# An attention kernel planned step by step: new load order for the first batch, a new rule for the weights' copies, the last pair of heads in two parts

## The chip, the cores and the metric

The kernel runs on one core of one Trainium2 chip. The metric is the device time of one execution in microseconds; the median over runs is compared. The core has a matrix engine (TensorE, PE), a vector engine (VectorE, DVE), a scalar engine (ScalarE, ACT), a general engine (GpSimd, POOL) and an engine that mainly issues transfers (SyncE, SP). Each works through its own instructions in order and waits for the others by semaphores.

## The reference

Two layers, eight batches. The first is attention over pooled keys and values, the second a mixture of four attention experts with causal scores, of which each token takes two:

```python
# q, k, v: (8, 8, 576, 64)
k_p = k.reshape(B, H, Sp, 8, D).mean(axis=3)      # 576 -> 72 rows
v_p = v.reshape(B, H, Sp, 8, D).mean(axis=3)
attn = softmax(scale * q @ k_p^T)
x = (attn @ v_p)  laid out as (B, S, H * D)        # (8, 576, 512)

logits = x @ w_gate                                # 4 experts, the best 2 are kept
for e in range(E):
    a = softmax(causal(scale * (x @ wq[e]) @ (x @ wk[e])^T))
    ye = a @ (x @ wv[e]) @ wo[e]
    out += w[:, :, e] * ye
```

## The kernel before

**Steps.** The kernel is written as a list of some 1390 small steps (`add`, line 1085), each with a name, an engine or a choice of two (ACT or DVE), the steps that it depends on and the PSUM bank that it takes. For each of eight batches (`plan_batch`, line 1171) there are:

- `ld`, `ln`: six loads, two halves each of k, q and v, issued by POOL (`load_half`, line 588) and landing later. Batch 0's loads are issued at the very start (`first`, line 1112); the table `LANDS` says when the planner takes them as landed.
- `pk`, `kp`, `kz`, `kt`, `kT`: k pooled by matmuls (line 655), copied, doubled (a "twin" copy), transposed, copied. `pv`, `vp`: v pooled and copied. `qm`, `qc`: q transposed on PE and copied; in batches 5 to 7 `qd`, `ql`, a DMA transpose, in its place.
- `am`, `ae`: scores of the first layer (line 722) and their exponentials on ACT (line 748). `an`, `af`, `al`: the same for the rows left over, which POOL puts in place (line 770, the "placing copies").
- `om`, `or`, `on`: the weighted sum (line 781), its reciprocal and its scaling into `xtm`. `xm`, `xc`: x transposed on PE; in batches 3 to 7 `xd`, `xl`, two DMA transposes.
- `jm`, `jc`: the experts' q and k (line 843), `vm`, `vc`: their v and the gate's logits (line 823). `ga` to `gc`: the gate.
- `bm`, `be`, `bk`: causal scores for a pair of experts in four parts (line 930), exponentials (line 940), masks on POOL (line 949).
- `bo`, `br`, `bg`, `bn`: the weighted sum of one expert over five chunks of 128 rows (line 964), reciprocal, gate, scaling into `osc`. `od`, `ol`: its DMA transpose into `oT`; in batch 7 `ot`, `oc` on PE and DVE or ACT.
- `ym`, `yc`, `ys`: the output product (line 1012), its copy (line 1023), its store by SP (line 1027). In batch 7 the second pair's part is a step of its own, `yn`.

Weights are loaded by POOL too (`wi`), and copied into the layout that PE needs (`wc`, line 1167): `wq`, `wk`, `wv` and `wg`.

**What sets the order.** `run_order` walks through the steps in planned time. PE takes its steps in the order of a table, `PE_ORDER`, which holds step numbers. The other engines take, of the steps that are ready in planned time, the one with the smallest number in the table `TURNS`. A third table, `ONLY`, ties some steps to ACT or DVE. Planned costs stand in `COST`; they decide only the order of the instructions. At most eight input loads are outstanding (`{"d": 8}`). Where nothing can be placed on PE for long, the planner puts in warm-up matmuls (line 1069). One rule concerns the placing copies: a twin copy (`kz`) goes to DVE only if planned time has passed the end of the last placing copy:

```python
and (e != "DVE" or st.kind != "kz" or now >= placed)
```

**DMA transposes.** All of them are issued by SP (`turn`, line 1101), behind the issue of the last input load, in order with the stores of the output.

Of the kernel before, what the change touches and what calls it, by code (L numbers as in the profile page):

```python
# [24 lines left out]
class Step:  # L25
# [23 lines left out]
SLOW = 4450  # L49
LANDS = {"k": (5700, 11500), "q": (8400, 13500), "v": (9950, 14900)}  # L50
# [9 lines left out]
    "wc": {"DVE": 440},  # L60
# [58 lines left out]
FIRST = {"bn": 0, "kz": 0, "kp": 1, "kT": 1, "qc": 1, "vp": 1, "xc": 0, "jc": 0, "vc": 1, "oc": 0, "yc": 0}  # L119
PE_ORDER = (  # L120
# [24 lines left out]
)  # L145
TURNS = (
# [364 lines left out]
def kernel(  # L511
# [22 lines left out]
    NC = 5  # L534
# [438 lines left out]
    def ob_rec(b, e, ob_ps):  # L973
        nc.vector.reciprocal(out=zb[:, b, :, e : e + 1], in_=ob_ps[:, :, HD : HD + 1])
# [842 lines left out]
```

## Time and profile before

| | |
|---|---|
| median of three runs | 175.83 us (175.18 to 177.23) |
| the profiled execution | 176.43 us |
| its span, from first to last instruction | 174.6 us |
| PE busy | 164.0 us (94%), of these 14.6 warm-up matmuls |
| DVE, ACT, POOL busy | 134.1, 131.6, 91.8 us |
| read from and written to HBM | 30.42 and 9.44 MB |
| mean granted clock of PE | 0.989 |

Busy time is the time in which an engine worked on at least one instruction; a share of the span is an average over stages with different limits. The chain of waits follows the work back from the last instruction. The granted clock is the part of PE's full clock that was allowed in a stretch. Times in the views are counted from the span's start.

### The profile page before, as it was taken

How to read it: one execution, taken by the hardware profiler on the slowest of the kernel's cores; microseconds unless marked ns; L12 is line 12 of the kernel's file. 1: busy time of each engine (PE TensorE's matmuls, PEld its weight loads, DVE VectorE, ACT ScalarE, POOL GpSimd, SP SyncE). 2: the span in 40 equal slices, each digit the busy share in tenths (PEclk: the TensorE clock that was granted, in tenths of full speed). 3: DMA queues.
4: the chain of work that ended last, by engine and by line, in shares of the span. 5: the costliest groups of instructions: out<-in, count | busy, mean ns of one | idle time of the engine just before them, and what ended most of it. 6: DMA issues, size and time to landing. Idle time of an engine off the chain costs nothing.

```text
span 174.6 us, 6224 instructions
## 1 busy us (share of the span) xinstructions
PE 164.0 (94%) x2419; PEld 127.9 (73%) x2432; DVE 134.1 (77%) x504; ACT 131.6 (75%) x229; POOL 91.8 (53%) x198
## 2 busy tenths in 40 slices
PE   7999995999999999999999999999999999999970
PEld 7898873888786987888877576778767676765550
DVE  5335877688789779999859799897788876979730
ACT  3035676469999996966899978999966799989820
POOL 8946639525897898930372760284230654564000
PEclk9999999699999999999999999999999999999999
DMA  2999999999999999999999999993839563557992
GB/s 33 176 198 202 207 198 203 204 205 205 205 140 196 205 205 207 192 167 199 167 181 156 238 264 230 243 140 66 155 103 219 122 220 101 156 101 215 379 348 82
DMA packets 49911, 32.45 MB, mean 186 GB/s; under 512 B 31188, under 2 KB 45268, under 8 KB 49876
## 3 DMA queue, kind: packets, MB, share of 16 engines
q0 software_dynamic: 15056, 15.21, 53.8%
q1 hardware_dynamic: 34820, 16.78, 42.0%
q8 instruction: 20, 0.33, 0.7%
q14 instruction: 15, 0.12, 0.2%
HBM read 30.42 MB, written 9.44 MB: 228 GB/s over the span
## 4 chain that ended last, share of the span: by engine, by line
PE 76%; DMA 13%; DVE 4%; POOL 2%; issue 2%; POOLq 0%; DVEq 0%; ACTq 0%
PE banks L843 19%; PE banks L823 11%; PE banks L964 9%; PE banks L1012 8%; PE banks L930 8%; DMA wvs<-in_moe_wv_dram 7%; PE banks L655 6%; PE banks L781 6%; DMA vb<-in_v_dram 5%; PE banks L722 4%; PE banks L709 2%; PE banks L810 1%; PE banks L1069 1%; PE banks L691 1%; POOL kb L596 1%
## 5 line engine op out<-in xcount | busy, mean ns | idle before, releaser
L940 ACT ACTIVATE etb<-banks 128x800 bf16<-128x800 f32 x64 | 51.1, 839 | 4.8 <-PE banks L930 4.3
L949 POOL TENSOR_SCALAR_AFFINE_SELECT etb<-etb 128x256 bf16<-128x256 bf16 (+1 forms) x80 | 30.4, 394 | 45.9 <-ACT etb L940 39.7
L748 ACT ACTIVATE eta<-banks 72x1024 bf16<-72x1024 f32 x32 | 37.4, 1209 | 5.1 <-PE banks L722 5.0
L798 DVE TENSOR_TENSOR xtm<-banks,za 128x256 bf16<-128x256 f32 (+1 forms) x80 | 31.0, 411 | 0.8 <-DVE za L793 0.2
L823 PE MATMUL banks<-wvg,xT 128*128 128x260 bf16 x160 | 23.0, 274 | 0.1
L843 PE MATMUL banks<-xT,wq_sb 128*128 128x384 bf16 (+1 forms) x128 | 21.4, 296 | 0.1
L770 POOL COPY eta<-etl 72x256 bf16<-72x256 bf16 (+1 forms) x18 | 19.8, 1334 | 2.8 <-ACT etl L759 2.5
L843 PE MATMUL banks<-xT,wk_sb 128*128 128x384 bf16 (+1 forms) x128 | 21.2, 291 | 0.1
L964 PEld LDWEIGHTS <-etb 128*128 128x128 bf16 x480 | 17.9, 97 | 3.4 <-issue 0.6
L781 PE MATMUL banks<-vpa,eta 72*128 72x65 bf16 x320 | 19.7, 196 | 0.3
L781 PEld LDWEIGHTS <-eta 72*128 72x128 bf16 x320 | 16.0, 100 | 5.1 <-issue 2.6
L964 PE MATMUL banks<-vau,etb 128*128 128x65 bf16 x480 | 19.4, 193 | 0.1
L930 PE MATMUL banks<-qTb,kTb 64*128 64x176 bf16 (+5 forms) x256 | 17.9, 248 | 0.3
L655 PEld LDWEIGHTS <-pm 64*72 64x72 bf16 x288 | 17.0, 111 | 0.5 <-issue 0.2
L1012 PE MATMUL banks<-wo_sb,oT 128*128 128x512 bf16 x59 | 17.1, 380 | 0.2
L1069 PE MATMUL banks<-warm 128*128 128x128 bf16 (+1 forms) x182 | 14.6, 244 | 1.5 <-DVE warm L1120 1.2
L823 PEld LDWEIGHTS <-xT 128*128 128x128 bf16 x160 | 13.9, 97 | 2.8 <-issue 0.8
L987 DVE TENSOR_TENSOR osc<-banks,gt 128x320 bf16<-128x320 f32 x31 | 15.0, 488 | 0.5
L793 DVE RECIPROCAL za<-banks 128x4 f32<-128x4 f32 (+1 forms) x80 | 12.1, 169 | 3.7 <-PE banks L781 2.2
L591 POOL DMA_DIRECT2D qb<-in_q_dram x16 | 11.7, 729 | 5.6 <-DMA vb<-in_v_dram 2.9
L1069 PEld LDWEIGHTS <-warm 128*128 128x128 bf16 (+1 forms) x182 | 12.9, 111 | 1.9 <-DVE warm L1120 1.1
L843 PEld LDWEIGHTS <-wk_sb 128*128 128x128 bf16 x128 | 10.9, 99 | 4.4 <-issue 1.4
(98 smaller groups left out, 288.2 us busy)
## 6 DMA issues: line engine op xcount, KB each, us to landing
out_dram<-y SPq DMA_DIRECT2D x36, 256.0 KB, 2.8
kb<-in_k_dram POOLq DMA_DIRECT2D x16, 288.0 KB, 7.6
qb<-in_q_dram POOLq DMA_DIRECT2D x16, 288.0 KB, 8.4
vb<-in_v_dram POOLq DMA_DIRECT2D x16, 288.0 KB, 8.1
wks<-in_moe_wk_dram POOLq DMA_DIRECT2D x1, 256.0 KB, 10.1
wvs<-in_moe_wv_dram POOLq DMA_DIRECT2D x1, 256.0 KB, 12.7
wqs<-in_moe_wq_dram POOLq DMA_DIRECT2D x1, 256.0 KB, 12.6
wo_sb<-in_moe_wo_dram POOLq DMA_DIRECT2D x1, 256.0 KB, 7.4
```

What stands on the lines that cost most here:

```text
L655: nc.tensor.matmul(out=jt[0:SK, m if len(ms) > 1 else 0, 0 : HQ * D], lhsT=pm[r, t, :], rhs=kv[r, t], start=(t == 0), stop=(t == TG - 1),)
L748: nc.scalar.activation(out=eta[i][:, p : p + 3 : 2, 0:S].rearrange("p x (g t) -> p g x t", t=TG)[:, :, :, lo : lo + 8], in_=jt[0:SK, 0:2, ...
L781: nc.tensor.matmul(out=oa_ps[:, h, :], lhsT=eta[i][:, p, c * 128 : (c + 1) * 128], rhs=vpa[iv][:, 4 * w + h, :], start=True, stop=True,)
L798: nc.vector.tensor_tensor(out=xtm[i][c // 3][0:n, :, c % 3].rearrange("p f (h e) -> p h f e", h=H)[:, 4 * w : 4 * w + 4], in0=oa_ps[0:n, : ...
L823: nc.tensor.matmul(out=v_ps[:], lhsT=xT[i][c // 3][:, f, c % 3 * 128 : (c % 3 + 1) * 128], rhs=wvg[:, f, :], start=(f == 0), stop=(f == NF ...
L843: nc.tensor.matmul(out=p_ps[:], lhsT=w_sb[:, f, g, :], rhs=xT[i][w][:, f, 0 : hi - lo], start=(f == 0), stop=(f == NF - 1),)
L930: nc.tensor.matmul(out=jt[:, ee, o : o + z - a], lhsT=kTb[i][r, g, kc * 128 : (kc + 1) * 128], rhs=qTb[i][r, g, a:z], start=True, stop=True,)
L940: nc.scalar.activation(out=etb[i][g][:, :, 400 * part : 400 * (part + 1)], in_=jt[:, :, 0:400], func=EXP, scale=B_SCALE,)
L949: nc.gpsimd.affine_select(out=et[:, :, o : o + w], in_=et[:, :, o : o + w], pattern=[[0, 2], [1, w]], compare_op=ISGE, fill=0.0, base=0, c ...
L964: nc.tensor.matmul(out=ob_ps[:, c, :], lhsT=etb[i][e // 2][:, e % 2, o : o + 128], rhs=vau[iv][:, kc, e, :], start=(kc == 0), stop=(kc == c),)
L1012: nc.tensor.matmul(out=y_ps[0:n], lhsT=oTs[g][:, c * 128 : c * 128 + n], rhs=wo_sb[:, g, :], start=(g == 0), stop=(g == NP - 1),)
L1069: nc.tensor.matmul(out=p_ps[:, j * 128 : (j + 1) * 128], lhsT=warm[r, :], rhs=warm[r, :], start=True, stop=True,)
```

## The change

Four things are changed, and the three tables are new with them.

1. **Batch 0's loads.** They were issued in the order k0, q0, v0, k1, q1, v1 (k0 is the first half of k) and are issued as k0, q0, k1, q1, v0, v1. `LANDS` has new planned times.
2. **The weights' copies.** `wc` was a DVE step; it may now run on ACT or DVE, and the rule on placing copies covers it.
3. **Batch 7's second pair of experts.** Its five chunks are done as chunks 0 to 2 and 3 to 4: weighted sum, reciprocal, gate, scaling, transpose and copy each in two steps. The first part waits for three of the four parts of the scores only, and the output's rows of chunks 0 to 2 wait for the first part only.
4. **Order.** `PE_ORDER`, `TURNS` and `ONLY` are replaced as a whole. Planned costs change in `SLOW` (a DMA transpose issued while loads are under way) and in the DMA's planned start.

```diff
-SLOW = 4450
-LANDS = {"k": (5700, 11500), "q": (8400, 13500), "v": (9950, 14900)}
+CUT = ((0, 3), (3, 5))
+SLOW = 3000
+LANDS = dict(zip((("k", 0), ("q", 0), ("k", 1), ("q", 1), ("v", 0), ("v", 1)), (5700, 8200, 9800, 11500, 13300, 14900)))
-    "wc": {"DVE": 440},
+    "wc": {"ACT": 1000, "DVE": 440},
-FIRST = {"bn": 0, ...}
+FIRST = {"wc": 1, "bn": 0, ...}
 PE_ORDER = (
-    20, 23, 30, 32, 50, 48, 42, 38, 24, 68, 27, 56, 34, 36, 40, 45, 52, 62, 54, 65, 59, 74, 80, 83,
+    20, 30, 24, 32, 23, 34, 50, 48, 42, 38, 36, 27, 56, 45, 54, 52, 59, 62, 40, 65, 74, 77, 80, 88,
...
-                and (e != "DVE" or st.kind != "kz" or now >= placed)
+                and (e != "DVE" or st.kind not in ("kz", "wc") or now >= placed)
...
-    def ob_mm(i, iv, e):
+    def ob_mm(i, iv, e, lo=0, hi=NC):
         ob_ps = small([128, NC, HD + 1], FP32)
-        for c in range(NC):
+        for c in range(lo, hi):
...
-    def ot_copy(oT, lo, ot_ps, cp):
-        cp(out=oT[:, lo : lo + S], in_=ot_ps[:].rearrange("p c x -> p (c x)")[:, 0:S])
+    def ot_copy(oT, lo, ot_ps, cp, at=0, to=S):
+        cp(out=oT[:, lo + at : lo + to], in_=ot_ps[:].rearrange("p c x -> p (c x)")[:, at:to])
...
-        for m in range(2):
-            for nm in "kqv":
-                load(nm, m)
+        for nm, m in LANDS:
+            load(nm, m)
...
-                lambda st=st, dst=dst: nc.vector.tensor_copy(out=dst, in_=st[:]),
+                lambda cp, st=st, dst=dst: cp(out=dst, in_=st[:]),
                 [("wl", 0, nm)],
+                share=1 if nm != "wg" else 0.2,
...
+            for lo, hi in CUT if (b, g) == (B - 1, NP - 1) else ((0, NC),):
+                p = (1,) if lo else ()
+                ks = range(4) if hi == NC else range(hi)
+                add(
+                    ("bo", b, e) + p,
+                    lambda e=e, lo=lo, hi=hi: ob_mm(i, iv, e, lo, hi),
+                    [("be", b, g, n) for n in ks]
+                    + [("bk", b, g, n, m) for n in ks for m in range(len(DIAG[n]))]
+                    + [("vc", b, c) for c in range(NC)],
+                    "s",
...
-                [("ym", last, c)] + [(z, b, 1) for z in ("oc", "ol") for b in (last - 1, last)],
+                [("ym", last, c), ("oc", last, 1), ("oc", last, 1, 1) if c > 2 else ("oc", last, 1)]
+                + [("ol", last - 1, 1)],
...
-            {"POOL": 6250, "DVE": 5300, "PE": 1000, "DMA": LANDS["v"][1] - 1200},
+            {"POOL": 6250, "DVE": 5300, "PE": 1000, "DMA": max(LANDS.values()) - 800},
```

`br`, `bg`, `bn` (`ob_rec`, `ob_gate`, `ob_norm`), `ot` and `oc` are split in the same way as `bo`; the final range check waits for the reciprocals of both parts.

Decoded to names, the new order's steps on PE right behind batch 0's first part are: pk of batch 1, three transposes of x, q's transposes, kt, `jm` q, `jm` k, the scores of batch 1, further `jm` steps. At the end, behind the last score step of batch 7, come: one output row of batch 6, `bo` of experts 2 and 3 (chunks 0 to 2), two rows, `ot` of the first pair, `bo` of expert 2 (chunks 3, 4), `ot` of the second pair, a row, and the five rows of batch 7 with the second parts in between.

More of the change, by code (lines that the diff above doesn't have):

```diff
@@ new lines @@
+    11: "DVE", 12: "DVE", 13: "DVE", 22: "DVE", 25: "DVE", 26: "DVE", 29: "ACT", 31: "ACT", 33:
+    "ACT", 35: "DVE", 37: "DVE", 87: "DVE", 89: "ACT", 93: "DVE", 95: "DVE", 97: "DVE", 105: "DVE",
+    107: "ACT", 109: "DVE", 113: "ACT", 119: "ACT", 121: "DVE", 177: "ACT", 181: "ACT", 185: "ACT",
+    189: "ACT", 206: "ACT", 210: "DVE", 214: "ACT", 261: "ACT", 263: "DVE", 265: "ACT", 267: "DVE",
+    269: "DVE", 275: "ACT", 279: "DVE", 281: "ACT", 285: "DVE", 287: "DVE", 289: "ACT", 293: "DVE",
@@ new lines @@
+    353: "DVE", 361: "DVE", 365: "DVE", 381: "DVE", 382: "DVE", 384: "DVE", 386: "ACT", 388: "ACT",
+    439: "ACT", 445: "DVE", 447: "ACT", 449: "ACT", 455: "ACT", 457: "ACT", 461: "ACT", 463: "ACT",
+    465: "ACT", 469: "ACT", 529: "DVE", 533: "DVE", 537: "DVE", 554: "DVE", 558: "ACT", 562: "DVE",
+    611: "DVE", 615: "DVE", 617: "DVE", 619: "DVE", 621: "DVE", 623: "ACT", 629: "DVE", 631: "ACT",
+    633: "DVE", 635: "ACT", 691: "DVE", 695: "ACT", 707: "ACT", 723: "DVE", 724: "DVE", 730: "ACT",
@@ L371 @@
+    "ACT", 1287: "ACT", 1289: "ACT", 1293: "ACT", 1295: "ACT", 1347: "DVE", 1351: "DVE", 1361:
+    "DVE", 1363: "DVE", 1367: "ACT", 1375: "ACT", 1379: "ACT",
 }
@@ L375, in run_order @@
     free = {e: start.get(e, 0) for e in ENGINES}
-    held = [0] * room["d"] + [LANDS[nm][m] for m in range(2) for nm in "kqv"]
+    held = [0] * room["d"] + list(LANDS.values())
     banks = [0] * 8
@@ L971, in ob_mm, with ob_rec, ob_gate, ob_norm @@
         return ob_ps
-    def ob_rec(b, e, ob_ps):
-        nc.vector.reciprocal(out=zb[:, b, :, e : e + 1], in_=ob_ps[:, :, HD : HD + 1])
-    def ob_gate(b, e, G):
-        gt = gtp.tile([128, NC, 1], FP32, name="gt", tag="gt", bufs=4)
-        nc.vector.tensor_mul(out=gt[:], in0=zb[:, b, :, e : e + 1], in1=G[:, :, e : e + 1])
+    def ob_rec(b, e, ob_ps, lo=0, hi=NC):
+        nc.vector.reciprocal(out=zb[:, b, lo:hi, e : e + 1], in_=ob_ps[:, lo:hi, HD : HD + 1])
+    def ob_gate(b, e, G, lo=0, hi=NC):
+        gt = gtp.tile([128, NC, 1], FP32, name="gt", tag="gt", bufs=6)
+        nc.vector.tensor_mul(
+            out=gt[:, lo:hi], in0=zb[:, b, lo:hi, e : e + 1], in1=G[:, lo:hi, e : e + 1]
+        )
         return gt
-    def ob_norm(e, gt, osc, ob_ps, cp=None):
+    def ob_norm(e, gt, osc, ob_ps, cp=None, lo=0, hi=NC):
         r = (e % 2) * HD
         if cp == nc.scalar.copy:
-            for c in range(NC):
+            for c in range(lo, hi):
                 nc.scalar.mul(osc[:, c, r : r + HD], ob_ps[:, c, 0:HD], gt[:, c])
@@ L987, in ob_norm, with ot_mm @@
         nc.vector.tensor_tensor(
-            out=osc[:, :, r : r + HD],
-            in0=ob_ps[:, :, 0:HD],
-            in1=gt[:].to_broadcast([128, NC, HD]),
+            out=osc[:, lo:hi, r : r + HD],
+            in0=ob_ps[:, lo:hi, 0:HD],
+            in1=gt[:, lo:hi].to_broadcast([128, hi - lo, HD]),
             op=MULT,
         )
-    def ot_mm(osc):
+    def ot_mm(osc, at=0, to=NC):
         ot_ps = small([128, NC, 128], BF16)
-        for c in range(NC):
+        for c in range(at, to):
             nc.tensor.transpose(out=ot_ps[:, c, :], in_=osc[:, c, :], identity=ident[:])
@@ L1478, in plan_batch @@
             g = e // 2
-            add(
-                ("bo", b, e),
-                lambda e=e: ob_mm(i, iv, e),
-                [("be", b, g, n) for n in range(4)]
-                + [("bk", b, g, n, m) for n in range(4) for m in range(len(DIAG[n]))]
-                + [("vc", b, c) for c in range(NC)],
-                "s",
-            )
-            def norm(cp=None, e=e, g=g):
-                if e % 2 == 0:
-                    T["osc", b, g] = work.tile([128, NC, 128], BF16, name=f"osc{g}", tag=f"osc{g}")
-                ob_norm(e, T["bg", b, e], T["osc", b, g], T["bo", b, e], cp)
@@ L1493, in plan_batch, with norm @@
-            add(("br", b, e), lambda e=e: ob_rec(b, e, T["bo", b, e]), [("bo", b, e)])
-            add(
-                ("bg", b, e),
-                lambda e=e: ob_gate(b, e, T["gc", b]),
-                [("br", b, e), ("gc", b)] + [("bn", b - 1, z) for z in range(E)],
-            )
-            add(
-                ("bn", b, e),
-                norm,
-                [("bo", b, e), ("bg", b, e), ("ot", old, g), ("ol", old, g)] + ([("bn", b, e - 1)] if e % 2 else []),
-                give=True,
-                kind="bl" if b == B - 1 else None,
-            )
+            for lo, hi in CUT if (b, g) == (B - 1, NP - 1) else ((0, NC),):
+                p = (1,) if lo else ()
+                ks = range(4) if hi == NC else range(hi)
+                part = 1 if hi - lo == NC else (hi * (hi + 1) - lo * (lo + 1)) / (NC * (NC + 1))
+                add(
[5 more added lines that the diff above has]
+                    "s",
+                    share=part,
+                )
+                def norm(cp=None, e=e, g=g, p=p, lo=lo, hi=hi):
+                    if e % 2 == 0 and not p:
+                        T["osc", b, g] = work.tile([128, NC, 128], BF16, name=f"osc{g}", tag=f"osc{g}")
+                    ob_norm(e, T[("bg", b, e) + p], T["osc", b, g], T[("bo", b, e) + p], cp, lo, hi)
+                add(
+                    ("br", b, e) + p,
+                    lambda e=e, p=p, lo=lo, hi=hi: ob_rec(b, e, T[("bo", b, e) + p], lo, hi),
+                    [("bo", b, e) + p],
+                    share=(hi - lo + 4) / (NC + 4),
+                )
+                add(
+                    ("bg", b, e) + p,
+                    lambda e=e, lo=lo, hi=hi: ob_gate(b, e, T["gc", b], lo, hi),
+                    [("br", b, e) + p, ("gc", b)] + [("bn", b - 1, z) for z in range(E)],
+                )
+                add(
+                    ("bn", b, e) + p,
+                    norm,
+                    [("bo", b, e) + p, ("bg", b, e) + p, ("ot", old, g), ("ol", old, g)]
+                    + ([("bn", b, e - 1)] if e % 2 else [])
+                    + ([("bn", b, e - e % 2)] if p else []),
+                    give=True,
+                    kind="bl" if b == B - 1 else None,
+                    share=(hi - lo) / NC,
+                )
@@ L1527, in plan_batch, with o_copy @@
             add(("ol", b, g), nothing, [("od", b, g)])
-        def o_copy(g, cp):
-            lo = oT_of(g)
-            ot_copy(T["oT", b // 2, g], lo, T["ot", b, g], cp)
+        at = {}
         for g in range(0 if b in O_DMA else NP):
-            add(
-                ("ot", b, g),
-                lambda g=g: ot_mm(T["osc", b, g]),
-                [("bn", b, 2 * g), ("bn", b, 2 * g + 1)],
-                "s",
-            )
-            add(
-                ("oc", b, g),
-                lambda cp, g=g: o_copy(g, cp),
-                [("ot", b, g)] + o_free + o_done(b - b % 2)[: b % 2 * 2],
-                give=True,
-            )
+            for lo, hi in CUT if (b, g) == (B - 1, NP - 1) else ((0, NC),):
+                p = (1,) if lo else ()
+                add(
+                    ("ot", b, g) + p,
+                    lambda g=g, lo=lo, hi=hi: ot_mm(T["osc", b, g], lo, hi),
+                    [("bn", b, 2 * g) + p, ("bn", b, 2 * g + 1) + p],
+                    "s",
+                    share=(hi - lo) / NC,
+                )
+                def o_copy(cp, g=g, p=p, lo=lo, hi=hi):
+                    if not p:
+                        at[g] = oT_of(g)
+                    ot_copy(T["oT", b // 2, g], at[g], T[("ot", b, g) + p], cp, lo * 128, min(hi * 128, S))
+                add(
+                    ("oc", b, g) + p,
+                    o_copy,
+                    [("ot", b, g) + p]
+                    + o_free
+                    + o_done(b - b % 2)[: b % 2 * 2]
+                    + ([("oc", b, g)] if p else []),
+                    give=True,
+                    share=(hi - lo) / NC,
+                )
         for c in range(4 + b % 2):
@@ L1591 @@
         )
-        add(("fz", last), range_end, [("fl", last)] + [("br", last, e) for e in range(E)])
+        add(
+            ("fz", last),
+            range_end,
+            [("fl", last)] + [("br", last, e) + p for e in range(E) for p in ((), (1,))],
+        )
         add(("fm", last), lambda: range_sum(T["fz", last]), [("fz", last)], "s")
```

27 lines of the change are left out of this document (8 added, 19 removed), and 455 rows, old and new, of tables (PE_ORDER, TURNS).

## The prediction

> **What bounds the kernel now.** I read the page first, then busy time by stretches, then the timeline and the chain of waits where the stretches showed a hole.
>
> ```profile
> span 174.6 us, 6224 instructions
> PE 164.0 (94%) x2419; PEld 127.9 (73%) x2432; DVE 134.1 (77%) x504; ACT 131.6 (75%) x229; POOL 91.8 (53%) x198
> PEclk9999999699999999999999999999999999999999
> GB/s 33 176 198 202 207 198 203 204 205 205 205 140 196 205 205 207 192 167 199 167 181 156 238 264 230 243 140 66 155 103 219 122 220 101 156 101 215 379 348 82
> L1069 PE MATMUL banks<-warm 128*128 128x128 bf16 (+1 forms) x182 | 14.6, 244 | 1.5 <-DVE warm L1120 1.2
> ```
>
> TensorE (PE) is busy 94% of the span, of which 14.6 us are warm-up matmuls. One slice, the eighth (30.5 to 34.9 us), has a lower granted clock. The busy time by stretches says where PE is not at its best:
>
> ```profile
> 21.00:28.30 7.30, 7.30 (x111) 5.44 (x108) 4.83 (x12) 6.03 (x9) 3.64 (x6) 1.00 1.33 201
> 28.30:30.30 2.00, 0.01 (x3) 0.01 (x2) 2.00 (x3) 0.80 (x1) 2.00 (x4) 1.00 1.22 204
> 30.30:33.70 3.40, 3.40 (x26) 2.47 (x26) 2.07 (x8) 1.50 (x2) 2.08 (x4) 0.58 1.23 204
> 33.70:36.00 2.30, 2.30 (x32) 1.97 (x30) 2.22 (x9) 0.94 (x3) 1.04 (x2) 0.88 1.20 204
> 33.70:86.90 53.20, 52.90 (x903) 44.54 (x901) 46.24 (x170) 44.08 (x73) 34.39 (x66) 0.99 1.18 192
> 86.90:160.00 73.10, 72.23 (x1020) 52.64 (x1030) 62.13 (x247) 64.67 (x120) 33.84 (x93) 1.00 0.79 167
> 160.00:167.00 7.00, 6.84 (x65) 3.51 (x65) 5.31 (x21) 6.18 (x15) 0.73 (x2) 1.00 1.00 366
> ```
>
> The columns are length, PE, weight loads, DVE, ACT, POOL, granted clock, DMA share, GB/s. From 33.7 to 160 us PE is busy 125.1 of 126.3 us: there the kernel is bound by PE's work in PE's fixed order. The one large hole is 28.3 to 30.3 us, and right behind it the clock is 0.58 for 3.4 us. The hole costs 1.99 us; the slow clock costs 3.4 x 0.42 = 1.4 us and, in the next stretch, 2.3 x 0.12 = 0.3 us. **Together 3.7 us.** What made the hole:
>
> ```profile
> 26.83 2.46 POOL L770 COPY eta<-etl 72x256 bf16<-72x256 bf16 x2
> 27.55 2.23 DVE L1167 COPY wvg<-wvs 128x1024 bf16<-128x1024 bf16 x1 [1.23 <-DMA wvs<-in_moe_wv_dram]
> 29.70 0.54 DVE L853 CAST kTb<-banks 128x384 bf16<-128x384 f32 x1
> 30.16 0.41 DVE L1167 COPY wq_sb<-wqs 128x1024 bf16<-128x1024 bf16 x1
> 30.29 0.38 PE banks L722 x3
> PE banks L722 <- DVE kTb L853: 2.0, 1, 2.0
> 14.78 12.74 DMA wvs<-in_moe_wv_dram
> ```
>
> DVE works in order. It stood 1.23 us at the copy of the v weights, whose load (issued 14.78) landed at 27.5. The copy then took 2.23 us while POOL's placing copies ran; the same copy of the q weights, with no placing beside it, took 0.41. A kTb copy stood behind it, and PE needed the bank that this copy empties. So 1.8 us of the hole is the collision and the rest the late landing.
>
> **A second wall.** Batches 3 to 7 are turned by DMA transposes that start only when the last input load has been issued; in this trace the first is issued at 78.83 us.
>
> ```profile
> 78.83 5.19 SPq L1110 DMA_TRANSPOSE xT<-xtm  x2
> xT<-xtm SPq DMA_TRANSPOSE x1, 6.4
> xT<-xtm SPq DMA_TRANSPOSE x1, 6.3
> 84.11 1.32 SPq L1110 DMA_TRANSPOSE qT<-qb  x1
> 86.88 1.06 PE L823 MATMUL banks<-wvg,xT 128*128 128x260 bf16 x8
> ```
>
> The first transpose lands at 78.83 + 6.4 = 85.2 us, the second, issued about 81.4, at 87.7. PE reaches the first matmul that uses one at 86.88, so the slack is 1.7 us now. A PE that comes 3.7 us earlier has none.
>
> **The change part by part.**
>
> *Load order.* The six halves of batch 0 stay six loads of the same size on the same queue, but k1 and q1 pass v0. Behind them, by the smaller keys in TURNS, POOL now issues k, q, wq, k, q, wk, v and then wv for batch 1, where it issued k, wk, q, k, q, v, v, wv, wq. Today PE stands on the q weights until their copy at 30.16; now q products can begin near 24 us. The price is on wk, sixth instead of second. POOL issues eight loads ahead, so each wait in its queue tells when a load landed:
>
> ```profile
> 20.52 0.70 POOL L591 DMA_DIRECT2D qb<-in_q_dram  x1 [1.02 <-DMA kb<-in_k_dram]
> 24.78 0.70 POOL L591 DMA_DIRECT2D qb<-in_q_dram  x1 [1.83 <-DMA vb<-in_v_dram]
> 23.93 0.81 PE L843 MATMUL banks<-xT,wk_sb 128*128 128x384 bf16 x4
> ```
>
> The fourth load landed at 20.5, the sixth at 24.8. So wk is copied at about 25.2 (24.8 + 0.41), and the first k product, now at 23.93, waits until then; PE has by then one q product (0.65 us) more behind it than today. Against today's course up to 28.3 us that is a wait of 0.6 us (1.3, the whole of 25.2 less 23.9, without the q product; bounds 0 and 1.3). What queues behind it on PE are batch 1's scores, and behind those ACT's exponentials (1.2 us each).
>
> *Weights' copies.* In the planner they now start on DVE only after the last placing copy has ended, as the small twin copies already did. All but one are tied to DVE, and wq may go to ACT, where the nearest row, half the size, is 0.59 us:
>
> ```profile
> L818 ACT COPY xT<-banks 128x512 bf16<-128x512 bf16 x8 | 4.6, 591 | 2.3 <-PE banks L810 2.2
> ```
>
> So it would cost ACT 0.6 to 1.2 us; ACT is free 1.27 us from 21 to 28.3 us and 1.2 us in the hole, which hides it. The 1.8 us of the collision goes, and with it the hole and the slow clock: **-3.7 us**, bounds 0 (it collides all the same) and -3.7.
>
> *New PE order.* I read PE_ORDER as names of steps. Up to the first step that needs a transpose the two orders hold the same steps but for pv of batch 6 (18 matmuls, about 1 us), which moves behind it, and five small ones. But the order alternates oftener between matmuls of 64 rows and of 128: 98 changes before, 108 after, all ten more ahead of the wall. Such a change has a price:
>
> ```profile
> 153.62 0.45 PE banks L930 x10
> 154.08 0.76 PE banks L843 x4
> 76.75 0.65 PE banks L843 x4
> ```
>
> Four matmuls right behind a 64-row group took 0.76 us, otherwise 0.65: 0.11 us each, **+1.1 us**. Ahead of the wall it is offset by pv's 1 us, which is paid after it.
>
> *The wall.* PE arrives 3.7 - 0.6 = 3.1 us earlier, at 83.8. When the first transpose lands depends on the loads. They ran at 205 GB/s but for dips; slice 12 (48 to 52 us, 140 GB/s) alone lost 4.37 x 65/205 = 1.4 us, that of 74 to 79 us (167) another 0.8. I read them as loads that waited for buffers, and PE now frees these 3 us sooner. I take 1.4 us earlier (bounds 0 and 2.2): landing at 83.8, as PE arrives. The second half lands 2.5 us after the first. PE's new order has three groups before it needs it, two of 0.65 and one of 0.45, 1.75 us together: **+0.75 us** wait (bounds 0 and, with the loads as late as today, 1.4 + 0.75 = 2.15).
>
> *Last pair in two parts.*
>
> ```profile
> 158.38 0.45 PE banks L930 x10
> 164.56 2.34 PE banks L1012 x10
> 166.92 0.69 DVE y L1023
> 159.19 9.97 SPq L1027 DMA_DIRECT2D out_dram<-y  x15
> 165.00:170.00 5.00, 4.06 (x43) 2.58 (x41) 1.59 (x4) 2.01 (x4) 0.00 (x0) 1.00 0.96 352
> L974 DVE RECIPROCAL zb<-banks 128x5 f32<-128x5 f32 x32 | 5.9, 186 | 3.0 <-PE banks L964 2.6
> L987 DVE TENSOR_TENSOR osc<-banks,gt 128x320 bf16<-128x320 f32 x31 | 15.0, 488 | 0.5
> ```
>
> PE has no hole in the tail, so finishing three fifths early shortens no PE time. It moves output products ahead: behind the last score step stand 9 output rows instead of 13. The stores fill the DMA (352 GB/s, share 0.96), and the last of fifteen is issued at 169.2, 1.5 us after the last copy ended (167.6). With four rows stored sooner I take half of this: **-0.7 us** (bounds -1.5 and, since each second part adds a reciprocal, a gate, a scaling and a copy, about 1.5 us of DVE for both heads, +0.5; DVE is free 1.7 of 7 us there, which hides it).
>
> **Sum.** -3.7 + 0.6 + 1.1 + 0.75 - 0.7 = -1.95 us, say -2.0. The profiled execution took 176.43 us (span 174.6 and 1.8 around it), so 174.4; the median of the runs is 0.6 lower, 175.83, so **173.8 us**.
>
> **The rivals.**
>
> *The loads hold the wall.* Speaks for it: DMA is busy 9 tenths through all of the loading, so earlier buffers need not bring earlier landings. Against: the dips. Then the wait is 2.15 instead of 0.75: -0.55, **175.3 us**, within 1%.
>
> *SP's queue turns the gain round (slower).* SP issues transposes back to back from 78.8 to 97 us, and in order. If two others (1.3 to 2.8 us each, say 2 x 1.65) come ahead of the second xT of batch 3, or one waits there for its input, PE waits 3.3 us more at the wall and the slow clock returns, 1.7 us as above: -1.95 + 5.0 = +3, **178.8 us**. It decides from a wait of some 2 us on, the length of today's hole. The keys in TURNS allow it: xT's second half no longer has one of the smallest. Against: of the entries with smaller keys most need steps that PE has not reached there. A wait of 2 us only, with the clock, gives +1.75, 177.6.
>
> The Trainium skill, "TensorE: Matmul & The Clock Gate", section "HAM oscillation — how this bites in real kernels", puts the limit at idle gaps above about 3.4 us. By that the clock would have held after today's 2.0 us, and here after anything shorter than the rule's gap; this case's rows say otherwise. By the page the 2 us wait would give 175.9 instead of 177.6.
>
> *The change doesn't do what it says.* The rule on placing copies lives in the planner's times. If the wv load lands late again, DVE's copy meets a placing copy as now: the 3.7 us stay, PE is not early at the wall (no 0.75), and with 1.1 - 0.7 it is +0.4, **176.2 us**. Against: wv keeps its place in the queue of loads and the order of DVE is now planned around the placing. For: the wait for wk moves batch 1's scores, and so its placing copies, 0.6 us closer to wv's landing.
>
> **How the numbers follow.** Forecast 0.43; loads hold the wall 0.23; SP's queue 0.25; no effect 0.09. This kernel's runs spread from 175.18 to 177.23, so about 1% (1.76 us, 174.07 and 177.59) can be told from no change. The forecast's own range is 171.7 (no wait for wk, loads 2.2 us earlier and so no wait at the wall, tail -1.5: -4.1) to 175.3, the rival with late loads. Of the forecast's 0.43 I put 0.05 above 174.07, of that rival's 0.23 I put 0.04 below it; SP's queue lies above 177.59 in the forms priced. So faster 0.43 - 0.05 + 0.04 = 0.42, same 0.05 + 0.19 + 0.09 = 0.33, slower 0.25. The range goes from 171.7 to 178.6: it leaves out the larger half of SP's rival and little else, not over 2 in 10.
>
> **What would show it.** Right: no PE hole over 1 us between 21 and 36 us and no slice with a granted clock under 8; the wv copy at about 0.4 us; the first matmul on a transposed xT near 84 to 85 us; fewer than 15 stores behind 159 us, relative to the end. Wrong: a PE hole of 2 us or more near 24 us (wk) or near 85 us with a slow slice behind it; or first transposes that land at 85 us or later, which leaves only the tail; or PE idle time of more than 2 us between 90 and 160 us, which nothing in the sum allows for.

## The result, and the profile after

The changed kernel took 176.03 us (median of 20 runs, 175.47 to 177.06) against 175.24 us for the kernel before (20 runs, 173.79 to 177.84). The ratio is 1.0071 with a 95% interval of 1.0048 to 1.0094: slower by 0.7%, inside the band of 1% and clear of no change. The forecast was 173.8 us, faster by 1.1%. The profiled execution took 176.86 us.

The page, first its lines of the span and of the granted clock:

```profile
span 175.1 us, 6249 instructions
PEclk9999999999999999999999999999999999999997
```

The slice with the low clock is gone from the head. Busy time by stretches, with the columns of the prediction (length, PE, weight loads, DVE, ACT, POOL, granted clock, DMA share, GB/s):

```profile
28.30:30.30 2.00, 2.00 (x22) 1.23 (x22) 1.00 (x4) 2.00 (x4) 2.00 (x3) 1.00 1.21 198
30.30:33.70 3.40, 3.40 (x60) 2.81 (x56) 2.08 (x8) 3.33 (x4) 3.06 (x5) 1.00 1.24 205
44.00:48.50 4.50, 3.69 (x58) 2.98 (x54) 3.72 (x7) 3.37 (x6) 4.18 (x6) 1.00 1.21 207
58.00:64.00 6.00, 4.23 (x80) 3.99 (x78) 5.50 (x8) 3.54 (x6) 4.95 (x7) 1.00 1.21 207
```

The hole of 28.3 to 30.3 us is filled: PE is busy 2.00 of 2.00 us where it was 0.01. Two new holes stand in its place: 44 to 48.5 us, 0.81 us idle, and 58 to 64 us, 1.77 us idle. The kernel before had neither:

```profile
40.00:50.00 10.00, 10.00 (x163) 8.41 (x162) 8.29 (x28) 9.51 (x18) 8.30 (x18) 1.00 1.21 205
60.00:70.00 10.00, 9.70 (x206) 8.37 (x203) 8.51 (x30) 8.49 (x13) 9.32 (x18) 1.00 1.22 206
```

What made the larger one is in the timeline of the changed kernel (start, length, engine, line, operation, output and input, idle time before it with what ended it):

```profile
59.25 2.37 DVE L913 TENSOR_TENSOR G<-W,rd 128x20 f32<-128x20 f32 x1
59.46 2.47 POOL L771 COPY eta<-etl 72x256 bf16<-72x256 bf16 x2
61.54 0.76 DVE L687 COPY kp<-kp 72x512 bf16<-72x512 bf16 x1
62.22 0.68 DVE L684 CAST kp<-banks 72x512 bf16<-72x512 f32 x1
62.95 0.81 PE L656 MATMUL banks<-vb,pm 64*72 64x256 bf16 x11 [1.77 <-DVE kp L684]
```

It is the event of the old hole with another victim. DVE's gate product `G = W * rd`, 128 x 20 numbers, took 2.37 us beside POOL's two placing copies, two copies of kp stood behind it on DVE, and PE needed the bank that the second of them empties. How far out of the ordinary this is, one tile's view shows: the number of products, and their shortest, middle and longest time in ns, in the changed kernel and then in the kernel before.

```profile
L913 DVE TENSOR_TENSOR G<-W,rd x8: 147/178/2371, 46.2 to 159.0; 128x20 f32<-128x20 f32 x8
```

```profile
L912 DVE TENSOR_TENSOR G<-W,rd x8: 159/174/201, 46.8 to 156.3; 128x20 f32<-128x20 f32 x8
```

The smaller hole is alike; here PE waits for DVE's copy of qT, which stands behind a stretched copy of kp and the product:

```profile
45.29 1.02 DVE L687 COPY kp<-kp 72x512 bf16<-72x512 bf16 x1
45.44 3.17 POOL L771 COPY eta<-etl 72x256 bf16<-72x256 bf16 x2
46.23 0.66 DVE L913 TENSOR_TENSOR G<-W,rd 128x20 f32<-128x20 f32 x1
47.42 0.42 PE L692 MATMUL banks<-ident,kp 72*128 72x72 bf16 x8 [0.81 <-DVE qT L716]
```

The planner's rule holds back the steps of kinds `kz` and `wc` while placing copies run; `gc`, the product, is free to start. In the old order no such product met a placing copy (the longest took 201 ns); in the new one two do.

### The profile page after: what moved, and what is told of

Its sections match the earlier page's. It is cut to its first block, busy times and chain, and to the rows that moved or that the text cites. A ratio compares the mean times of both kernels' runs of the same rounds, so it can differ in the third digit from the quotient of the medians.

```text
span 175.1 us, 6249 instructions
## 1 busy us (share of the span) xinstructions
PE 163.6 (93%) x2432; PEld 126.0 (72%) x2432; DVE 132.5 (76%) x507; ACT 135.4 (77%) x229; POOL 92.8 (53%) x198
## 4 chain that ended last, share of the span: by engine, by line
PE 75%; DVE 12%; DMA 6%; POOL 2%; issue 2%; POOLq 0%; DVEq 0%
PE banks L844 17%; PE banks L824 10%; PE banks L1015 9%; PE banks L656 8%; PE banks L931 7%; PE banks L965 7%; PE banks L782 6%; DMA vb<-in_v_dram 6%; PE banks L723 3%; PE banks L1072 2%; PE banks L710 2%; DVE xtm L799 2%; DVE osc L990 2%; PE banks L811 1%; DVE G L913 1%
## 5 line engine op out<-in xcount | busy, mean ns | idle before, releaser
L771 POOL COPY eta<-etl 72x256 bf16<-72x256 bf16 (+1 forms) x18 | 20.7, 1362 | 4.8 <-ACT etl L760 4.8
L782 PE MATMUL banks<-vpa,eta 72*128 72x65 bf16 x320 | 20.7, 194 | 0.1
L844 PE MATMUL banks<-xT,wk_sb 128*128 128x384 bf16 (+1 forms) x128 | 20.7, 286 | 0.0
L1015 PE MATMUL banks<-wo_sb,oT 128*128 128x512 bf16 x72 | 20.6, 380 | 0.0
L844 PE MATMUL banks<-xT,wq_sb 128*128 128x384 bf16 (+1 forms) x128 | 20.6, 286 | 0.0
L990 DVE TENSOR_TENSOR osc<-banks,gt 128x320 bf16<-128x320 f32 (+2 forms) x34 | 15.5, 462 | 0.5
L794 DVE RECIPROCAL za<-banks 128x4 f32<-128x4 f32 (+1 forms) x80 | 12.7, 169 | 3.6 <-PE banks L782 2.8
L1026 ACT COPY y<-banks 128x512 f32<-128x512 f32 x24 | 13.7, 587 | 1.8 <-PE banks L1015 1.3
L1072 PE MATMUL banks<-warm 128*128 128x128 bf16 (+1 forms) x182 | 14.0, 241 | 1.2 <-DVE warm L1123 1.2
```

Of the source, the lines that this page charges most:

```text
L771: nc.gpsimd.tensor_copy(out=eta[i][:, 2 * lo : 2 * hi, 0:S].rearrange("p (m z) (g t) -> p m z g t", z=2, t=TG)[:, :, w, :, t], in_=etl[:, ...
L782: nc.tensor.matmul(out=oa_ps[:, h, :], lhsT=eta[i][:, p, c * 128 : (c + 1) * 128], rhs=vpa[iv][:, 4 * w + h, :], start=True, stop=True,)
L844: nc.tensor.matmul(out=p_ps[:], lhsT=w_sb[:, f, g, :], rhs=xT[i][w][:, f, 0 : hi - lo], start=(f == 0), stop=(f == NF - 1),)
L1015: nc.tensor.matmul(out=y_ps[0:n], lhsT=oTs[g][:, c * 128 : c * 128 + n], rhs=wo_sb[:, g, :], start=(g == 0), stop=(g == NP - 1),)
```

## The experiments

The theory was that these two collisions are the whole of the loss; against it stood that the time is lost elsewhere and that the two holes only take up waits which would come anyway. The runs were made on several chips, on which the kernel before had medians from 174.87 to 175.24 us, so versions are compared best by their ratios to it.

**The gate product on GpSimd.** There it runs in POOL's own order and cannot meet a placing copy.

```diff
-        nc.vector.tensor_mul(
+        nc.gpsimd.tensor_tensor(
             out=G[:], in0=..., in1=...,
+            op=MULT,
```

> The changed kernel with one instruction per batch moved: the gate's last product (G = W * rd, eight in all, 0.18 us each when alone) is issued on POOL instead of DVE, at the same place of the plan. In the changed kernel it took 2.37 us at 59.3 us and 0.66 at 46.2, beside POOL's placing copies, and PE then stood 1.8 and 0.8 us. Theory A (the lead of 2.2 us that the changed kernel has at 44 us is lost to these two collisions on DVE's queue): both holes of PE shrink to under 0.5 us, the step that is reached at 86.7 us is reached at about 84.7, and the time is 174 to 174.8 us, ratio to the kernel before 0.993 to 0.998. Rival B (the loads' landing and the DMA transposes behind it hold the wall near 85 us): the holes vanish but PE waits near 85 us, and the ratio stays 1.003 to 1.008.

Measured: 173.98 us (12 runs, 173.17 to 174.63), ratio to the kernel before 0.994 (0.991 to 0.997). That is 2.05 us under the changed kernel by the medians and, by the ratios (1.0071 less 0.994), 2.3 us. Its timeline at the same place, and its busy time in two windows and at the wall:

```profile
59.36 1.22 DVE L687 COPY kp<-kp 72x512 bf16<-72x512 bf16 x1
59.48 0.23 POOL L913 TENSOR_TENSOR G<-W,rd 128x20 f32<-128x20 f32 x1
59.64 3.24 POOL L771 COPY eta<-etl 72x256 bf16<-72x256 bf16 x2
60.50 0.67 DVE L684 CAST kp<-banks 72x512 bf16<-72x512 f32 x1
```

```profile
40.00:50.00 10.00, 9.79 (x141) 7.53 (x138) 7.95 (x26) 9.48 (x15) 8.42 (x16) 1.00 1.21 206
60.00:70.00 10.00, 9.95 (x196) 8.77 (x191) 8.88 (x29) 9.17 (x16) 10.00 (x17) 1.00 1.17 196
80.00:100.00 20.00, 20.00 (x304) 15.72 (x303) 15.70 (x54) 18.71 (x32) 8.04 (x20) 1.00 1.21 171
```

Theory A holds (the time came out 0.02 us under its range): without the two collisions the same order is faster than both kernels. What was lost stays lost: ACT has the same 229 instructions in the same order in both kernels, of which the 57th starts at 55.72 us in the changed kernel and at 55.67 here, the 65th at 63.45 and 61.73, the last at 167.51 and 165.44. The kp copy that now meets the placing copies is only stretched, to 1.22 us, and the second copy ends 1.7 us earlier than in the changed kernel (61.17 against 62.90).

**Is the collision there every time?** The changed kernel, profiled again:

> The changed kernel unchanged, profiled a second time. Theory A (the gate product beside the placing copies near 59 us collides in every execution): it takes 2 us or more again instead of 0.18, PE loses about 2 us more between 56 and 64 us than in e1, time 175.5 to 177 us. Rival B (it comes and goes, as the hole of the kernel before does): product under 0.5 us, PE without a wait over 1 us there, time 174 to 174.8 us.

Measured: 176.0 us (a single run).

```profile
59.06 2.37 DVE L914 TENSOR_TENSOR G<-W,rd 128x20 f32<-128x20 f32 x1
```

```profile
PE banks L657 <- DVE kp L685: 1.8, 1, 1.8
```

The product took the same 2.37 us. Theory A holds in both profiles, and two versions below that keep the product on DVE in this order (another finish, another place of the range check) show it at 2.37 and 2.38 us. The slowest of the 12 runs without it (174.63) lies under the fastest of the changed kernel (175.47).

**The old hole alone.** In the kernel before, the copy of the v weights was put behind that of the q weights, and nothing else was changed:

```diff
+            def w_copy(nm=nm, st=st, dst=dst):
+                if nm == "wv":
+                    late.append((st, dst))
+                    return
+                nc.vector.tensor_copy(out=dst, in_=st[:])
+                if nm == "wq":
+                    for s, d in late:
+                        nc.vector.tensor_copy(out=d, in_=s[:])
```

> The kernel before with one copy moved: the copy of the v weights is issued on DVE right behind the copy of the q weights, no longer ahead of the kTb copy on which PE waits; load order, PE order and everything else as before. Theory A (the hole at 28.3 us is this copy, late and blocked by the placing copies, at the head of DVE's queue): the hole of 2.0 us and the slow clock behind it go, with at most 0.6 us left at the q weights; if nothing takes it back, PE is 3 us early from 36 us on and the ratio is 0.982 to 0.988. Rival B (the wall of loads and transposes near 85 us holds): PE is early until 80 us and then waits, ratio 0.992 to 1.0. Rival C (the hole comes from the late landing alone): hole over 1 us stays, ratio 0.995 to 1.0.

Measured: 174.93 us (12 runs), ratio 0.9995 (0.9955 to 1.0035). In the list of what PE waited for (total, times, longest):

```profile
PE banks L843 <- DVE wq_sb L1171: 0.9, 1, 0.9
```

```profile
80.00:100.00 20.00, 19.14 (x249) 13.46 (x244) 14.34 (x52) 17.74 (x31) 9.91 (x24) 1.00 1.14 169
```

The hole shrank to 0.9 us and no slow clock followed it, yet the time did not move; rival B is the nearest. Part of the gain is paid at the second wall (0.86 us idle from 80 to 100 us, above, where the profiled execution of the kernel before had 0.20, below). The rest raised the question whether that execution, 176.43 us, stands for the kernel at all.

```profile
80.00:100.00 20.00, 19.80 (x277) 15.23 (x276) 16.13 (x60) 18.30 (x35) 8.44 (x23) 1.00 1.15 185
```

**The kernel before, again.** Three more profiles of it:

> The kernel before, unchanged, profiled a second time: the -3.7 us of the forecast were read from one execution of 176.43 us, above most of this kernel's times. Theory A (the hole is there in every execution, the slow clock behind it is not): the PE hole near 28 us is again 1.5 to 2.0 us, but the clock behind it stays at 0.9 or more, and the time is 174.5 to 175.2 us. Rival B (the whole of it is typical): hole 2.0 us, granted clock near 0.58 for 3.4 us behind it, time 176 to 176.5 us. Rival C (the hole itself is rare): no PE idle over 1 us between 26 and 36 us, time under 174.5 us.

> The same program once more, as a third profile of the kernel before. Theory A: hole of 1.5 to 2.0 us, clock 0.9 or more behind it, 174.5 to 175.2 us. Rival B: hole of 2.0 us and a clock near 0.58 for 3.4 us, 176 to 176.5 us. Rival C: no hole over 1 us, under 174.5 us.

> The kernel before once more, for how often its hole near 28 us is long. Of three profiled executions two had a hole of 2.0 us with a clock of 0.50 behind it (176.43 and 176.91 us), one a hole of 0.46 us and no slow clock (173.91). Theory A (the hole is long or short by the moment at which the copy of the v weights meets the placing copies, and the time follows it): a hole of 1.7 to 2.2 us goes with a slow clock and 176 us or more, one under 1.3 us with no slow clock and 175.5 us or less. Rival B (the time does not follow the hole): a long hole under 175.5 us, or a short one above 176 us.

Measured: 176.91, 173.91 and 174.23 us. For the first, the second and the third of them in turn, the copy of the v weights, the placing copies and PE's wait from the timeline, and the page's line of the clock:

```profile
26.67 3.32 DVE L1167 COPY wvg<-wvs 128x1024 bf16<-128x1024 bf16 x1 [0.36 <-DMA wvs<-in_moe_wv_dram]
27.03 2.47 POOL L770 COPY eta<-etl 72x256 bf16<-72x256 bf16 x2
30.50 0.43 PE L722 MATMUL banks<-qT,kpT 64*72 64x256 bf16 x3 [2.19 <-DVE kTb L853]
```

```profile
PEclk9999999699999999999999999999999999999998
```

```profile
26.35 2.81 POOL L771 COPY eta<-etl 72x256 bf16<-72x256 bf16 x2
26.64 1.35 DVE L1168 COPY wvg<-wvs 128x1024 bf16<-128x1024 bf16 x1
29.68 0.50 PE L844 MATMUL banks<-xT,wq_sb 128*128 128x192 bf16 x4 [0.37 <-DVE wq_sb L1168]
```

```profile
PEclk9999999999999999999999999999999999999996
```

```profile
26.05 2.48 POOL L771 COPY eta<-etl 72x256 bf16<-72x256 bf16 x2
26.06 2.95 DVE L1168 COPY wvg<-wvs 128x1024 bf16<-128x1024 bf16 x1 [0.22 <-DMA wvs<-in_moe_wv_dram]
29.52 0.38 PE L723 MATMUL banks<-qT,kpT 64*72 64x256 bf16 x3 [1.69 <-DVE kTb L854]
```

```profile
PEclk9999999999999999999999999999999999999999
```

The first is rival B's case, with all that the prediction was read from; the second is rival C's, a short hole without the slow clock. The third lies on the edge, a hole of 1.69 us where theory A began at 1.7, but its time, under 175.5 us, is that of rival B: the time does not follow the hole alone. So the collision is in all four profiled executions, but its length depends on which of the two engines comes first and by how much, and the slow clock behind it came in two of four: after 1.99 and 2.19 us of idle time, not after 1.69. That clock is most of what parts 176.4 and 176.9 us from 174.2: some 3.4 us of it at half speed make 1.7 us. In the first and the third of these profiles, one stretch (length, PE, granted clock, DMA share, GB/s):

```profile
32.00:34.00 2.00, 2.00 (x17) 0.50 1.21 207
```

```profile
32.00:34.00 2.00, 2.00 (x35) 1.00 1.21 207
```

**The slow clock by itself.** Six warm-up matmuls were put ahead of the score matmuls that stand in the hole:

```diff
-    def a_mm(kpT, qT, y):
+    def a_mm(kpT, qT, y, warmers=0):
         jt = joint()
+        for j in range(warmers):
+            nc.tensor.matmul(
+                out=jt[:, (TG * y + y % 2) % 2, 0:128],
+                lhsT=warm[0:64, :], rhs=warm[0:64, :], start=True, stop=True)
```

> The kernel before with six more warm-up matmuls on PE just ahead of the score matmuls that stand in the hole near 28 us; nothing that the hole waits for is touched. In four profiled executions of the kernel before, holes of 1.99 and 2.19 us were followed by a clock of 0.50 for some 3.4 us (176.4 and 176.9 us), holes of 1.69 and 0.46 us were not (174.2 and 173.9). Theory A (an idle time of some 2 us sets the clock down, and that alone makes the slow quarter of this kernel's executions): PE's longest idle time there is 1.6 us or less, no slow clock, no time above 175.9 us where 17 of 66 of the kernel before were, ratio 0.994 to 0.999. Rival B (the slow quarter comes from elsewhere, the filling only costs its own 0.6 us): a quarter of the times still above 175.9 us, ratio 1.000 to 1.004.

Measured: 175.2 us (12 runs, 174.19 to 177.11), ratio 0.999 (0.9957 to 1.0022). PE's longest wait there was 1.42 us and no slice had a low clock, as theory A said, but two of the twelve times lie above 175.9 us, and the profiled execution, without any slow clock, took 176.02. Neither theory is upheld, and two of twelve cannot be told from a quarter. The profiled execution shows one other source: its last copy of an output row ended at 166.04 us and its span 8.15 us later, where the four profiles of the kernel before have 7.0 to 7.2. So some 1 us of its lateness lies in the stores and the end behind PE's work; why stays open.

**The two-part finish.** It was taken out of the changed kernel, and put alone into the kernel before; in both the order around it was rewritten by hand.

```diff
-CUT = ((0, 3), (3, 5))
+CUT = ((0, 5),)
```

> The changed kernel with the last pair of heads finished whole, in place of the second parts in the order; the rest as changed. Theory A (the second parts cost the tail: their chain of small DVE steps ends about 1.0 us after PE has run out of work, which the profile of the changed kernel shows at 164.7 to 165.7 us): ratio 1.002 to 1.006, that is 0.2 to 0.9 us faster than the changed kernel. Rival (finishing in two parts pays, as it lets output rows start earlier): ratio 1.009 to 1.013.

> The kernel before with the two-part finish of the last pair of heads alone; loads, weights' copies and the order up to the last pair as before. Theory A (the two-part finish is worth what its removal cost the changed kernel, 1.2 us, or what the forecast gave it, 0.7 us): ratio 0.993 to 0.996, and from PE's last score steps to the end of the span some 1 us less than in the kernel before. Rival B (it pays only with the rest of the new order; the second parts' reciprocals, gates and copies on VectorE eat it): ratio 0.999 to 1.003.

Measured: without it 177.66 us (6 runs), ratio 1.0139 (1.0091 to 1.0186), 1.2 us over the changed kernel by the ratios (1.6 by the medians); put into the kernel before, 175.81 us (12 runs), ratio 1.0036 (1.0003 to 1.0068). It does not help there. Without it PE stands and warms up behind the last chain of DVE and ACT, and the DMA is busy only 0.59 (the timeline and the busy time of that kernel):

```profile
164.73 1.05 PE L918 MATMUL banks<-ident,osc 128*128 128x128 bf16 x5 [0.20 <-ACT osc L906]
165.61 0.94 PE L990 MATMUL banks<-warm 128*128 128x128 bf16 x14
```

```profile
165.00:170.00 5.00, 5.00 (x59) 3.56 (x60) 1.45 (x4) 2.64 (x7) 0.00 (x0) 1.00 0.59 215
```

In the kernel before with the finish in two parts the stores already fill the DMA, and there is no gap to close:

```profile
160.00:165.00 5.00, 4.99 (x49) 2.60 (x47) 4.27 (x18) 3.47 (x9) 0.00 (x0) 1.00 0.99 363
```

The first run's theory A falls to its rival, the second's to its own. An order made for two parts loses by one part, and an order made for one loses by two. Since both tails were mended by hand, neither run gives the price of the finish itself.

**The range check last.** In the changed kernel its four small DVE operations stand ahead of the last `osc`; its last PE step was put behind the last output product, and its DVE operations were given a late key.

> The changed kernel with the last part of the range check (four small DVE reductions and compares, 0.4 us, which stand between the last gate and the last scaling on DVE) moved behind everything else, its matmul last on PE. Theory A (these are on the path that ends last): the last output product starts 0.3 to 0.4 us earlier, but the check itself now ends last, so the ratio is 1.004 to 1.008, within 0.3 us of the changed kernel. Rival (the stores' transfers set the end): no change, 1.005 to 1.009. A ratio above 1.010 would say that the check's own chain is the longer one.

Measured: 176.63 us (12 runs), ratio 1.0062 (1.0022 to 1.0102), within its interval of the changed kernel's 1.0071; it lies in the range of both theories and does not part them. Two of the 12 runs took 174.75 and 174.83 us, near the version without the collisions; they have no profile, so whether a collision was missing in them stays open. The same on top of the gate product on GpSimd:

> The kernel of e1 (gate product on GpSimd) with the end of the range check put behind the last output products, as in e4. Theory A (in the tail the stores bind: the DMA is busy 1.00 of 160 to 165 us in e1): no difference from e1, ratio to the kernel before 0.992 to 0.996. Rival B (the range check's four VectorE operations ahead of the last osc delay the end by 0.45 us): ratio 0.990 to 0.992.

Measured: 174.36 us (12 runs, 173.43 to 176.38), ratio 0.9962 (0.9924 to 1.0), no better than 0.994 without it. Of this run's two theories A is the nearer. The small operations in front cost nothing that these runs can show.

**The new load order.** From the version with the gate product on GpSimd, batch 0's loads and its first steps were put back into the old order:

```diff
-LANDS = dict(zip((("k", 0), ("q", 0), ("k", 1), ("q", 1), ("v", 0), ("v", 1)), ...))
+LANDS = dict(zip((("k", 0), ("q", 0), ("v", 0), ("k", 1), ("q", 1), ("v", 1)), ...))
```

> The kernel of e1 (the changed kernel with the gate product on GpSimd), with batch 0's loads and its first steps in the old order (k0, q0, v0, k1, q1, v1). Theory A (the new load order costs the 0.5 to 1.1 us by which PE is behind the old kernel up to 26 us): that lag is gone, and the time is 0.5 to 0.8 us below e1's: ratio to the kernel before 0.990 to 0.992. Rival B (the lag comes from the weights' order and the longer PE order, not from batch 0's loads): ratio 0.994, as e1. Rival C (the new load order is what saves time): ratio 0.997 or more.

Measured: 174.05 us (9 runs), ratio 0.9937 (0.9909 to 0.9964). That is 0.994 again, as rival B said, though the interval does not shut out theory A's 0.992: the load order of batch 0 is worth nothing that can be seen.

## Why the prediction was wrong

**The step that failed** is the one on the weights' copies: "The 1.8 us of the collision goes, and with it the hole and the slow clock". It went at the place that was looked at, and came back at another. The rule covers two kinds of step; every other DVE step was left free, and the prediction asked of the new order only where PE's steps fall, never which DVE step now falls beside a placing copy. The sum lacks a term of +2.0 to 2.3 us (176.03 less 173.98 by the medians, 1.0071 less 0.994 by the ratios; 0.81 + 1.77 = 2.58 us of idle PE by the trace, against 0.21 + 0.05 with the product moved).

**Its size was wrong too.** The -3.7 us are 1.99 of hole and 1.7 of slow clock, read from one execution. Of four profiled ones two had the slow clock. In the other two the hole alone was there: 1.69 us in one, and in the other 0.46 us in two stalls, the longer of 0.37. The subtraction of 0.6 us from the profiled time to the median did not mend this: the time of 176.43 held a loss that two of the four do not have. So even without the new collisions the gain falls short: 0.994 of 175.24 is 1.05 us (0.5 to 1.6 by the interval), where 1.95 was forecast. The terms below are held against the execution of 174.23 us (hole of 1.69, no slow clock), a fairer start for a trace, though itself 0.8 us under the median of that chip's runs.

**The terms, against that start.**

- *Hole:* -1.7, as the wait that has gone. In the head all that was foretold is there. Each weight's copy is free of placing copies, on DVE in 0.43 us (0.4 predicted) and, for q, on ACT in 1.05 us (0.6 to 1.2 predicted):

```profile
19.42 1.05 ACT L1169 COPY wq_sb<-wqs 128x1024 bf16<-128x1024 bf16 x1
24.50 0.43 DVE L1169 COPY wk_sb<-wks 128x1024 bf16<-128x1024 bf16 x1
27.57 0.43 DVE L1169 COPY wvg<-wvs 128x1024 bf16<-128x1024 bf16 x1 [1.09 <-DMA wvs<-in_moe_wv_dram]
```

- *Wait for wk, +0.6, and ten more switches between row forms, +1.1.* wk's copy began at 24.50 us (24.8 predicted), but no wait for it is seen: PE was busy 10.00 of 10 us from 20 to 30 in the changed kernel, 9.73 in the version without collisions. What is seen is longer work in the same matmuls. Up to the end of the last output product PE was busy, in the execution of 174.23 us and in the version without collisions:

```profile
0.00:164.69 164.69, 160.38 (x2400) 124.24 (x2400) 134.06 (x501) 131.37 (x229) 92.29 (x198) 1.00 0.99 188
0.00:165.36 165.36, 162.59 (x2410) 124.63 (x2411) 129.18 (x499) 134.54 (x228) 95.07 (x206) 1.00 1.02 189
```

PE is idle 1.5 us less (4.31 and 2.77) and busy 2.2 us longer. Ten more warm-up matmuls are 0.8 of these 2.2 us (11.64 and 12.42 us in all, which the sum had not); the other 1.4 are near the 1.1 of the switches. That the switches are the cause was not tested. The other profiles go the same way: 160.9 us busy in the kernel before's execution of 173.91 us, 162.2 and 162.7 in the two of the changed kernel.

- *The wall, +0.75:* nothing. PE was busy 20.00 of 20 us from 80 to 100, in the version without collisions as well. That the first matmul on a transposed xT came at 84.83 us ("near 84 to 85 us" predicted) is luck: PE had lost 2.6 us in the two new holes by then. Without them that matmul came at 82.79 us (84.58 in the kernel before's execution of 174.23 us), behind a first transpose issued at 77.45. In the changed kernel the transposes came in time too:

```profile
79.49 3.24 SPq L1113 DMA_TRANSPOSE xT<-xtm  x2
84.83 1.06 PE L824 MATMUL banks<-wvg,xT 128*128 128x260 bf16 x8
```

- *Tail, -0.7:* not isolated. Fourteen stores stand behind 159 us instead of fifteen, as predicted, but that count goes with how late an execution is (11 in the one of 174.23 us), and the DMA is busy 0.97 of 160 to 167 us:

```profile
159.23 9.45 SPq L1030 DMA_DIRECT2D out_dram<-y  x14
```

```profile
160.00:167.00 7.00, 6.84 (x73) 3.38 (x69) 5.55 (x27) 6.08 (x11) 1.47 (x4) 1.00 0.97 354
```

The span ends 7.72 us behind the last output product in the execution of 174.23 us, 7.62 and 7.03 in the two profiles of the changed kernel and 6.81 in the version without collisions: 0.1 to 0.9 us sooner, in single executions. No run shows that the finish in two parts is what does it.

So from 174.23 us to the version without collisions the traces have -1.5 of idle time, +2.2 of work and -0.9 behind the last product, together -0.2, which is what the two spans differ by (172.4 and 172.2). The two new collisions put 2.0 to 2.3 us on top.

**The rivals.** SP's queue did not hold the wall, and the loads did not either. The rival that the change doesn't do what it says gave 176.2 us, near the measured time, for another reason: it had the v weights' copy collide again, which did not happen. (Its sum also leaves out the +0.6 for wk without saying that the hole would take it up.) The rule did its work for the kinds that it names. The signs that were listed for a right forecast came true (for the clock, in the head), and the forecast was wrong all the same. The list of what would prove it wrong looked for idle time near 24, near 85 and from 90 to 160 us, and none from 36 to 80, where it was.

## What to carry to other kernels

When a change removes a collision between two engines by moving one of its victims, list every other instruction of that engine that the new order can put beside the same culprit, and look above all for those whose follower on the in-order queue frees a bank that TensorE needs. Putting the small instruction on the culprit's own engine (here the product on GpSimd, 2 us for one line) rules that collision out whatever the order, but not the next one of its kind. And before a gain is read off a profile, see how the profiled execution stands among the times: a loss that only some executions have is not there to be won back in the others.

## What the runs showed of the hardware

**A small product can stand for more than ten times its length.** 128 x 20 numbers took 2.37 us instead of 0.18, from 0.21 us ahead of two placing copies until nearly their end (61.62 against 61.93). A copy of 72 x 512 with one input, in the same place, took 1.22 us instead of 0.76, and there the placing copies grew from 2.47 to 3.24 us. The Trainium skill, "SBUF — State Buffer", section "SBUF: two separate sides", has the rule for this: VectorE, in a two-port mode or with two SBUF inputs, and GpSimd need one port pair, and whichever starts first keeps it for its whole instruction. The trace agrees that the one waits the other out; it does not agree that the shown start decides, since the product's start lies 0.21 us ahead of the placing copy's, and the v weights' copy at 26.67 us lost to a placing copy that began at 27.03.

**The clock fell after idle times of PE of about 2 us, counted in steps of 3.41 us.** In the clock records of all fourteen traces the changes lie 3.41 us or a multiple of it apart. From full clock it fell to 0.50 behind each of the 17 such steps in which PE had been idle for 1.87 us or more (at the old hole, once at a late load of q, and at the end of the kernel), and behind none with 1.77 us or less. The step that holds the old hole of 1.99 us, and the one that holds the new hole of 1.77 (length, PE, granted clock, DMA share, GB/s):

```profile
27.44:30.85 3.41, 1.42 (x21) 1.00 1.22 204
60.54:63.95 3.41, 1.64 (x33) 1.00 1.21 207
```

The clock of the next step was 0.50 behind the first and 1.00 behind the second. The hole of 1.69 us fell on a border between two steps, 0.82 and 0.87 us, so it says little of the limit: where a hole falls counts as well as its length. The slow clock lasted one step at the old hole and two at the late load (1.88 us idle, in the version with the product on GpSimd and the range check last, an execution of 176.38 us). The Trainium skill's page "TensorE: Matmul & The Clock Gate", section "HAM oscillation — how this bites in real kernels", gives gaps above about 3.4 us; by these rows less suffices.
